# Sliding-window attention and a mixture of experts on one core: bf16 attention in 128-key blocks, tokens sorted by expert through a DRAM scatter, and the feed-forward of the chosen expert only, in 256-token tiles

## The chip, the core and the metric

One core of a Trainium2 chip runs the whole program. The time is device microseconds (us) of one execution. The engines are TensorE (PE for matmuls, PEld for weight loads), VectorE (DVE), ScalarE (ACT), GpSimd (POOL) and SyncE (SP); POOL and SP also issue transfers, POOL those that cast or go through an index. "Kernel before" and "kernel after" are the two sides of the diff.

## The reference

Attention with a window of 32 keys to either side runs over 8 batches of 8 heads, 576 positions and 64 columns. Its output is laid out as 4608 tokens of 512 columns. Each token then takes one of 8 experts by a gate, to whose logits a bias by the token's modality (0 or 1) is added.

```python
def _attn_ref(q, k, v):                       # q, k, v: (8, 8, 576, 64)
    scores = scale * np.matmul(q, k.transpose(0, 1, 3, 2))
    mask = np.abs(pos[:, None] - pos[None, :]) <= 32
    attn = softmax(np.where(mask, scores, -1e9))
    return np.matmul(attn, v)

def _moe_ref(x, modality_id, w_gate, modality_bias, w1, w2):   # x: (4608, 512), w1: (8, 512, 1024)
    logits = x @ w_gate + modality_bias[modality_id]
    e_idx = np.argmax(logits, axis=1)
    gate_w = softmax(logits)[np.arange(N), e_idx]
    for e in range(8):
        mask = e_idx == e
        h = np.maximum(x[mask] @ w1[e], 0.0)
        out[mask] = gate_w[mask, None] * (h @ w2[e])
    return out
```

The inputs are a fixed draw: random q, k, v, weights and biases, and modality 0 or 1 for each token at random.

## The kernel before

**Attention** loops over batch and head (L98, L99). For one head, k and q come in five pieces of 128 positions (L111, L117), are transposed on TensorE in fp32 (L113, L119) and copied to bf16 by VectorE (L114, L120). Then nine blocks of 64 queries follow, each against at most 128 keys: a score matmul (L137), scaling and mask on VectorE (L142), the exponent on ScalarE (L146), a load of the block's v rows on GpSimd's queue with a column of ones beside it (L151, L152), the output matmul with the sum in its last column (L155), a reciprocal and a scaling on VectorE (L158, L160), a transpose back (L165), a copy (L167) and a store of 64 x 64 values to `xT_dram` (L171).

**Gate and feed-forward** start when the attention's pools are closed. All experts' weights are then loaded to SBUF by two casting transfers on GpSimd's queue (L196, L200). Nine tiles of 512 tokens follow (L204). A tile is loaded transposed (L207), its logits are four groups of four matmuls of 8 columns (L214), and some fifteen small VectorE steps make the gate weight for the chosen expert and zero for the others (L219 to L260). Then each of the eight experts runs on the whole tile: 32 matmuls of 512 columns into `hT_ps` (L268), the relu on ScalarE (L272), 32 into `y_ps` (L277), and a multiply-add into `y_acc` on VectorE (L282, L287).

The code is written in program order, and a scheduler orders each engine's instructions when the kernel is built, with the pools' buffers and the data as its limits. Each engine then has a list of its own, with waits on semaphores in it.

## Time and profile before

| what | us |
|---|---|
| median of three executions | 1835.68 |
| lowest and highest | 1833.14, 1836.53 |
| span of the profiled execution, first to last instruction | 1834.9 |
| TensorE, VectorE, ScalarE, GpSimd busy in it | 1555.3, 789.7, 499.5, 311.4 |

The span lies 0.8 us under the median of the three, and the profiled execution has no time of its own beside its span, so that is all that can be said of what lies around it. A group of instructions is given by its line, engine, operation, tiles and shape, with its count, busy time, the mean length of one, and the idle time of the engine just before them with what ended it. Matmuls are pipelined: the busy time of a group divided by its count is the distance from one to the next, and the mean length of one is longer. PEclk is TensorE's granted clock as a share of full speed.

### The profile page before, as it was taken

The page shows a single profiled execution, that of the slowest core. Times are in us where ns is not written, and L with a number is a line of the kernel's source. Part 1 is how long each engine was busy: PE and PEld are TensorE (multiplying, and loading weights), DVE is VectorE, ACT ScalarE, POOL GpSimd, SP SyncE. Part 2 cuts the span into 40 slices and gives each one's busy share as a digit, 9 for nine tenths or more (in the row PEclk, how much of TensorE's full clock was granted, in tenths as well). Part 3 has the DMA queues.
Part 4 walks back from the last instruction along what each step waited for, and adds up shares of the span by engine and source line. Part 5 has one row for each costly group of instructions (what it writes and reads, how often), then busy time and mean ns, then how long its engine had stood idle before and what let it go on. Part 6 is the DMA issues. An engine that isn't in the chain of part 4 may idle for free.

```text
span 1834.9 us, 25930 instructions
## 1 busy us (share of the span) xinstructions
PE 1555.3 (85%) x7025; PEld 723.3 (39%) x7120; DVE 789.7 (43%) x4477; ACT 499.5 (27%) x1189; POOL 311.4 (17%) x596
## 2 busy tenths in 40 slices
PE   6777777777777777335999999999999999999999
PEld 3333333333333333112444444444444444444444
DVE  6667766766666676601212222313223231231322
ACT  1121112111111111121333333333333333333333
POOL 4443434443433444200000000000000000000000
PEclk9999999999999999997999999999999999999999
DMA  3343333333333333694000100101001010000000
GB/s 43 46 57 46 46 45 54 47 46 45 45 45 45 45 46 46 95 210 78 1 35 1 35 0 1 35 0 35 1 0 35 1 35 0 17 19 1 24 1 23
DMA packets 239198, 65.52 MB, mean 36 GB/s; under 512 B 217552, under 2 KB 230352, under 8 KB 239056
## 3 DMA queue, kind: packets, MB, share of 16 engines
q0 software_dynamic: 93744, 26.00, 13.4%
q1 hardware_dynamic: 145312, 37.88, 9.3%
q8 instruction: 59, 0.97, 0.2%
q14 instruction: 83, 0.68, 0.1%
HBM read 75.56 MB, written 14.16 MB: 49 GB/s over the span
## 4 chain that ended last, share of the span: by engine, by line
PE 68%; DMA 19%; issue 6%; DVE 5%; another core or an unknown queue 1%; POOL 1%; ACT 0%; SPq 0%; POOLq 0%; DVEq 0%; ACTq 0%
PE hT_ps L268 27%; PE y_ps L277 27%; DMA vaug<-in_v_dram 7%; DMA xT_dram<-oT 4%; PE tps L119 3%; PE o_aug L155 3%; PE tps L113 3%; DMA tmp<-in_q_dram 3%; PE oT_ps L165 3%; DMA w_all<-in_moe_w_dram 2%; PE sc L137 2%; DMA tmp<-in_k_dram 2%; DVE o_sb L160 1%; DVE recip L158 1%
## 5 line engine op out<-in xcount | busy, mean ns | idle before, releaser
L268 PE MATMUL hT_ps<-xT_sb,w_all 128*128 128x512 bf16 x2259 | 510.4, 380 | 41.5 <-DMA w_all<-in_moe_w_dram 38.7
L272 ACT ACTIVATE hT_sb<-hT_ps 128x512 bf16<-128x512 f32 x576 | 343.8, 597 | 695.0 <-PE hT_ps L268 653.7
L277 PE MATMUL y_ps<-w_all,hT_sb 128*128 128x512 bf16 x2254 | 507.1, 380 | 25.2 <-DMA w_all<-in_moe_w_dram 22.9
L287 DVE SCALAR_TENSOR_TENSOR yacc<-y_ps,mask_ge,yacc 128x512 f32<-128x512 f32 x252 | 189.2, 751 | 674.6 <-PE y_ps L277 662.9
L151 POOL DMA_DIRECT2D vaug<-in_v_dram x576 | 303.8, 530 | 445.6 <-DVE recip L158 140.3
L268 PEld LDWEIGHTS <-w_all 128*128 128x128 bf16 x2304 | 224.3, 98 | 310.7 <-DMA w_all<-in_moe_w_dram 38.3
L277 PEld LDWEIGHTS <-hT_sb 128*128 128x128 bf16 x2304 | 225.8, 98 | 296.6 <-issue 26.0
L146 ACT ACTIVATE exps<-exps 128x64 bf16<-128x64 bf16 (+1 forms) x576 | 144.9, 255 | 605.4 <-DVE exps L142 281.4
L165 PE MATMUL oT_ps<-ident,o_sb 64*64 64x64 f32 x576 | 174.9, 307 | 48.4 <-DVE o_sb L160 32.3
L155 PE MATMUL o_aug<-vaug,exps 128*64 128x65 bf16 x576 | 141.1, 249 | 78.7 <-DMA vaug<-in_v_dram 52.1
L119 PE MATMUL tps<-ident,tmp 128*64 128x128 f32 (+1 forms) x320 | 126.6, 396 | 39.7 <-DMA tmp<-in_q_dram 23.7
L167 DVE CAST oT<-oT_ps 64x64 bf16<-64x64 f32 x576 | 121.8, 211 | 81.3 <-DMA xT_dram<-oT 38.7
L160 DVE TENSOR_SCALAR o_sb<-o_aug,recip 64x64 f32<-64x64 f32 x576 | 153.6, 268 | 0.1
L113 PE MATMUL tps<-ident,tmp 128*64 128x128 f32 (+1 forms) x320 | 127.3, 398 | 27.5 <-DVE kT_sb L114 10.5
L137 PE MATMUL sc<-qT_sb,kT_sb 64*128 64x64 bf16 (+1 forms) x576 | 134.1, 235 | 6.2 <-DVE exps L142 4.0
L155 PEld LDWEIGHTS <-exps 128*64 128x64 bf16 x576 | 72.4, 127 | 164.5 <-issue 84.1
L158 DVE RECIPROCAL recip<-o_aug 64x1 f32<-64x1 f32 x576 | 89.3, 156 | 87.1 <-PE o_aug L155 81.1
L165 PEld LDWEIGHTS oT_ps<-ident,o_sb 64*64 64x64 f32 x576 | 75.9, 132 | 118.9 <-DVE o_sb L160 70.5
L120 DVE CAST qT_sb<-tps 64x128 bf16<-64x128 f32 (+1 forms) x320 | 84.2, 263 | 35.4 <-PE tps L119 22.3
L114 DVE CAST kT_sb<-tps 64x128 bf16<-64x128 f32 (+1 forms) x320 | 84.0, 262 | 24.5 <-PE tps L113 20.4
L142 DVE SCALAR_TENSOR_TENSOR exps<-sc,mask_mid 128x64 bf16<-128x64 f32 x448 | 92.6, 207 | 0.5 <-PE sc L137 0.2
L137 PEld LDWEIGHTS <-kT_sb 64*128 64x128 bf16 (+1 forms) x576 | 64.5, 114 | 65.9 <-issue 48.5
(46 smaller groups left out, 311.1 us busy)
## 6 DMA issues: line engine op xcount, KB each, us to landing
w_all<-in_moe_w_dram POOLq DMA_DIRECT2D x2, 8192.0 KB, 64.9
xT_dram<-oT SPq DMA_DIRECT2D x576, 8.0 KB, 1.8
out_dram<-yacc SPq DMA_DIRECT2D x36, 256.0 KB, 2.0
tmp<-in_k_dram SPq DMA_DIRECT2D x256, 32.0 KB, 1.9
tmp<-in_q_dram SPq DMA_DIRECT2D x256, 32.0 KB, 1.9
vaug<-in_v_dram POOLq DMA_DIRECT2D x512, 16.0 KB, 2.1
xT_sb<-xT_dram SPq DMA_DIRECT2D x9, 512.0 KB, 3.8
tmp<-in_k_dram SPq DMA_DIRECT2D x64, 16.0 KB, 2.0
```

The source lines that it names most:

```text
L113: nc.tensor.transpose(tps[:, :sl], tmp[:sl, :], ident[:sl, :sl])
L119: nc.tensor.transpose(tps2[:, :sl], tmp2[:sl, :], ident[:sl, :sl])
L137: nc.tensor.matmul(sc[:sk, :], kT_sb[:, ks:ke], qT_sb[:, qs:qs + QB], start=True, stop=True)
L146: nc.scalar.activation(exps[:sk, :], exps[:sk, :], mybir.ActivationFunctionType.Exp)
L151: nc.gpsimd.dma_start(vaug[:sk, :D], vbh[ks:ke, :])
L155: nc.tensor.matmul(o_aug[:], exps[:], vaug[:], start=True, stop=True)
L160: nc.vector.tensor_scalar(out=o_sb[:], in0=o_aug[:, :D], scalar1=recip[:], scalar2=None, op0=mybir.AluOpType.mult,)
L165: nc.tensor.transpose(oT_ps[:], o_sb[:], ident[:QB, :QB])
L268: nc.tensor.matmul(hT_ps[:], w1_all[:, e, kd, mi * P:(mi + 1) * P], xT_sb[:, kd, :], start=(kd == 0), stop=(kd == n_kd - 1),)
L272: nc.scalar.activation(hT_sb[:, mi, :], hT_ps[:], mybir.ActivationFunctionType.Relu)
L277: nc.tensor.matmul(y_ps[:], hT_sb[:, kf, si * P:(si + 1) * P], w2_all[:, e, kf, :], start=(kf == 0), stop=(kf == n_kf - 1),)
L287: nc.vector.scalar_tensor_tensor(out=y_acc[si][:], in0=y_ps[:], scalar=mask_ge[:, si, e:e + 1], in1=y_acc[si][:], op0=mybir.AluOpType.mult ...
```

## The change

Both halves are rewritten; no function of the computation is left as it was.

**Attention.** q and k of four heads are loaded at once as 96 partitions of six positions each and cast to bf16, q on GpSimd and k on ScalarE. v comes in five blocks of 128 keys for all heads and is cast on GpSimd. A pass takes two heads: six transposes for q and six for k into one PSUM buffer, copied by VectorE (q) and ScalarE (k); ten score matmuls of 192 or 96 queries against blocks of 128 keys into two PSUM tiles `sA` and `sB`; two exponents on ScalarE straight from PSUM; two multiplications by a mask of ones and zeros on VectorE; eighteen output matmuls of 65 columns into `oA` and `oB`, with a reciprocal and a normalisation each. The result goes to a row tile `xt` of 128 tokens by 544 bf16 columns.

**Routing**, once a batch: the rows are transposed, the logits and the chosen expert worked out for 5 x 128 slots (a batch's 576 tokens and 64 empty ones) in one set of small steps, ranks within the expert come from matmuls with a triangle and ones, and five indirect transfers on GpSimd's queue scatter the rows to a DRAM table `scr` with 4608 places for each expert. A row carries its gate weight and its token number. After batch 0 the weights of two experts that the batch used are loaded into two slots of SBUF.

**Feed-forward.** A table worked out on VectorE gives for each of 25 tile numbers the expert, whether its weights differ from those in the slot, and the first row; even and odd numbers run from the two ends of the list. 19 tiles are written out, six more stand in a conditional block that runs when the count asks for them. A tile of 256 tokens loads its rows by a register's address, transposes them, runs both matrices of its one expert, scales by the row's gate weight and scatters 2 x 128 rows to `out` with two indirect transfers. Its weight loads carry a condition from the table.

```diff
-        for b in range(B):
-            for h in range(H):
-                for si in range(n_ks):
-                    nc.sync.dma_start(tmp[:sl, :], kbh[s0:s1, :])
-                    nc.tensor.transpose(tps[:, :sl], tmp[:sl, :], ident[:sl, :sl])
-                    nc.vector.tensor_copy(kT_sb[:, s0:s1], tps[:, :sl])
...
-                for qi in range(n_qb):
-                    nc.tensor.matmul(sc[:sk, :], kT_sb[:, ks:ke], qT_sb[:, qs:qs + QB], start=True, stop=True)
...
-                    nc.gpsimd.dma_start(vaug[:sk, :D], vbh[ks:ke, :])
...
-        w1_all = moe_w_pool.tile([P, E, n_kd, F], BF16, tag="w1")
-        for nt in range(n_nt):
...
-            for e in range(E):
...
+        tc.tile_pool(name="ps_s", bufs=1, space=bass.MemoryType.PSUM) as ps_s,
+        tc.tile_pool(name="ps_o", bufs=1, space=bass.MemoryType.PSUM) as ps_o,
+        tc.tile_pool(name="ps_t", bufs=1, space=bass.MemoryType.PSUM) as ps_t,
+        tc.tile_pool(name="ps_m", bufs=1, space=bass.MemoryType.PSUM) as ps_m,
     ):
         for b in range(B):
...
+                    if nm == "q":
+                        nc.gpsimd.tensor_copy(o_ap, i_ap)
                     else:
+                        nc.scalar.copy(o_ap, i_ap)
...
+                nc.sync.dma_start(f_[:], v[b, :, s0:s0 + P, :].rearrange("h s d -> s h d"))
+                nc.gpsimd.tensor_copy(vt[:, j, :, 0:D], f_[:])
...
+                for src, dst, eng in ((qb[g], qT[:, 32:32 + S], "v"), (kb[g], kT[:], "a")):
+                    tp = ps_t.tile([P, S], BF16, tag="tp")
+                    for i in range(R):
+                        nc.tensor.transpose(tp[:, SP_ * i:SP_ * (i + 1)],
+                                            src[:, i, D * l:D * l + P], ident[0:SP_, 0:SP_])
...
+                    nc.scalar.activation(pt[:, :, o0:o0 + wd], s_t[:, :, 0:wd], ACT.Exp, scale=scale)
+                    w2_ = 512 if o0 == 0 else 384
+                    nc.vector.tensor_tensor(
+                        out=pt[:, :, o0:o0 + w2_], in0=pt[:, :, o0:o0 + w2_],
+                        in1=mask[:, o0:o0 + w2_].unsqueeze(1).to_broadcast([P, 2, w2_]), op=ALU.mult)
...
+            for m in range(NM):
+                tp = ps_t.tile([P, n_kd, P], BF16, tag="tp")
+                for kd in range(n_kd):
+                    nc.tensor.transpose(tp[:, kd, :], xr[:, m, P * kd:P * kd + P], ident[:])
+                xT = rt.tile([P, n_kd, P], BF16, tag="xT")
+                nc.vector.tensor_copy(xT[:], tp[:])
...
+            for m in range(NM):
+                nc.gpsimd.indirect_dma_start(
+                    out=scr[:], out_offset=bass.IndirectOffsetOnAxis(ap=di[:, m:m + 1], axis=0),
+                    in_=xi[:, m, :], in_offset=None, bounds_check=E * N - 1, oob_is_err=False)
+            if b == 0:
...
+                for i in range(2):
+                    e_r = reg(sp_i[0:1, i:i + 1], [ET.Pool], 0, E - 1)
+                    load_w(1, i, e_r)
+                    load_w(2, i, e_r)
...
+        def stage_load(i):
+            r_r = reg(tab[0:1, 2, i:i + 1], [ET.SP], 0, E * N - TT)
+            xg = xgp.tile([P, 2, ROW // 2], I32, tag="xg")
+            nc.sync.dma_start(xg[:], scr[bass.ds(r_r, TT), :].rearrange("(s p) c -> p s c", p=P))
...
+        def weights(i):
+            e_r = reg(tab[0:1, 0, i:i + 1], [ET.Pool], 0, E - 1)
+            c_r = reg(tab[0:1, 1, i:i + 1], [ET.Pool], 0, 1)
+            load_w(1, i % 2, e_r, cond=(c_r == 1))
...
+                nc.gpsimd.indirect_dma_start(
+                    out=out, out_offset=bass.IndirectOffsetOnAxis(ap=ix[:, s:s + 1], axis=0),
+                    in_=ys[:], in_offset=None, bounds_check=N - 1, oob_is_err=False)
...
+            if x_ + 1 < n:
+                stage_load(tiles[x_ + 1])
+                wr = weights(tiles[x_ + 1])
+            up(i)
+            if x_:
+                down(tiles[x_ - 1])
+            if x_ + 1 < n:
+                weights2(tiles[x_ + 1], wr)
...
+        ffn(list(range(n_base)), pools)
+        with tc.If(n_tiles > n_base):
+            ffn(list(range(n_base, NTILE)), pools)
```

Where instructions stand now is shown at three places. Names end in a number that tells copies apart, and DMASW, DMAHW, DVE, PE and Activation behind "waits" are the semaphores that an instruction waits on; DMASW are those of transfers issued by GpSimd, several of them in turn.

The first place is TensorE in the middle of attention. Before, scores (`sc`) and outputs (`o_aug`) of one head's blocks and transposes alternate:

```order
L165 MATMUL oT_ps_12340<-ident_61,o_sb_12338 64x64 [waits DVE_49]
L137 LDWEIGHTS kT_sb_12255
L137 MATMUL sc_12421<-qT_sb_12256,kT_sb_12255 128x64 [waits DVE_49]
L165 MATMUL oT_ps_12359<-ident_61,o_sb_12357 64x64 [waits DVE_49]
L155 LDWEIGHTS exps_12366 [waits DMASW2_49,Activation_49]
L155 MATMUL o_aug_12372<-vaug_12369,exps_12366 64x65 [waits PE_49]
```

Now, at the end of a pass (`pt1` is the pass's masked exponent, `kT_1175` the next pass's k):

```order
L288 LDWEIGHTS pt1_157
L288 MATMUL oB_1151<-vt0_159,pt1_157 128x65
L295 LDWEIGHTS pt1_157
L295 MATMUL oB_1151<-vt0_159,pt1_157 64x65
L272 LDWEIGHTS kT_1175
L272 MATMUL sA_1192<-qT1_155,kT_1175 128x192
```

All scores of the next pass but its first now stand behind the last output matmul of this one.

The second place is GpSimd in the middle of attention. Before, it only issues the blocks' v loads:

```order
L151 DMA vaug_2095<-in_v_dram 128x64 [waits DMASW5_49,DVE_49,PE_49]
L151 DMA vaug_2115<-in_v_dram 96x64 [waits DMASW6_49,DVE_49,PE_49]
L151 DMA vaug_2187<-in_v_dram 128x64 [waits DMASW7_49,PE_49]
L151 DMA vaug_2206<-in_v_dram 128x64 [waits DMASW0_49,PE_49]
L151 DMA vaug_2225<-in_v_dram 128x64 [waits DMASW1_49,DVE_49,PE_49]
```

Now, at a batch's end, with casts of q and v for later batches among and behind the five row scatters:

```order
L364 DMA scr_66<-xt0_161,di_2062 36864x272 [waits DMASW0_49,DVE_49]
L233 CAST c__2822<-f__2820 96x4x6x64 [waits DMAHW3_49,PE_49,Pool_49]
L364 DMA scr_66<-xt0_161,di_2062 36864x272 [waits DMASW1_49]
L364 DMA scr_66<-xt0_161,di_2062 36864x272 [waits DMASW2_49]
L364 DMA scr_66<-xt0_161,di_2062 36864x272 [waits DMASW3_49]
L233 CAST c__2830<-f__2828 96x4x6x64 [waits DMAHW7_49,PE_49,Pool_49]
L364 DMA scr_66<-xt0_161,di_2062 36864x272 [waits DMASW4_49]
L242 CAST vt1_160<-f__2836 128x8x64 [waits DMAHW0_49,PE_49,Pool_49]
```

Each scatter waits for the landing of the one before it, and the casts behind them stand in the same list.

The third place is GpSimd in the feed-forward. Before, its last transfers are the two weight loads, and nothing of the tiles is on it:

```order
L151 DMA vaug_14470<-in_v_dram 128x64 [waits DMASW4_49,DVE_49,PE_49]
L151 DMA vaug_14490<-in_v_dram 96x64 [waits DMASW5_49,DVE_49,PE_49]
L196 DMA w1_all_14532<-in_moe_w1_dram 128x32x1024 [waits DMAHW2_49,DMAHW1_49,DMAHW3_49,DMAHW0_49,DMAHW4_49,DMASW7_49,DMAHW5_49,DMASW6_49,DMAHW6_49,DMASW0_49,DMAHW7_49,DVE_49,Activation_49]
L200 DMA w2_all_14534<-in_moe_w2_dram 128x64x512
L318 UNCONDITIONAL_BRANCH
```

Now, one tile's share of it:

```order
L185 TENSOR_LOAD tab_3235 x2
L178 REGISTER_ALU x2
L178 ISA
L178 DMA w1_1_151<-in_moe_w1_dram 128x4x1024 [waits DMASW4_49]
L509 DMA out_0_dram<-ys_3642,ix_3617 4608x512 [waits DMASW2_49,DVE_49]
L509 DMA out_0_dram<-ys_3723,ix_3712 4608x512 [waits DMASW5_49,DVE_49]
L181 REGISTER_ALU x2
L181 ISA
L181 DMA w2_1_153<-in_moe_w2_dram 128x8x512 [waits DMASW7_49,PE_49]
```

Register loads, two conditional weight loads and two output scatters a tile have come to GpSimd, and each scatter waits for a landing.

## Rows read from the trace of the kernel before

**Rows 1.** The page: its first line, and busy time by engine.

```profile
span 1834.9 us, 25930 instructions
...
PE 1555.3 (85%) x7025; PEld 723.3 (39%) x7120; DVE 789.7 (43%) x4477; ACT 499.5 (27%) x1189; POOL 311.4 (17%) x596
```

**Rows 2.** Three stretches: length, each engine's busy us (instructions), PEclk, DMA share, GB/s.

```profile
0.00:752.00 752.00, 553.71 (x2362) 267.19 (x2362) 517.57 (x3643) 145.93 (x576) 306.41 (x593) 1.00 0.38 46
752.00:845.00 93.00, 20.93 (x111) 9.88 (x113) 17.00 (x133) 12.21 (x25) 4.97 (x3) 0.89 1.05 181
845.00:1835.00 990.00, 980.64 (x4555) 446.26 (x4646) 255.16 (x703) 341.36 (x588) 0.00 (x0) 1.00 0.04 14
```

**Rows 3.** The chain that ended last, 752 to 850 us: start, length, what.

```profile
758.55 45.52 DMA w_all<-in_moe_w_dram
...
821.58 22.87 another core or an unknown queue
```

**Rows 4.** Groups of TensorE, then a piece of the whole chain of waits.

```profile
L268 PE MATMUL hT_ps<-xT_sb,w_all 128*128 128x512 bf16 x2259 | 510.4, 380 | 41.5 <-DMA w_all<-in_moe_w_dram 38.7
...
L268 PEld LDWEIGHTS <-w_all 128*128 128x128 bf16 x2304 | 224.3, 98 | 310.7 <-DMA w_all<-in_moe_w_dram 38.3 <-issue 11.3
...
L214 PE MATMUL logits_ps<-wg_sb,xT_sb 128*128 128x8 bf16 x144 | 6.5, 167 | 8.2 <-DVE logits L219 7.8 <-DVE oT L167 0.3
...
997.29 6.95 PE hT_ps L268 x32
```

**Rows 5.** Groups of ScalarE.

```profile
L272 ACT ACTIVATE hT_sb<-hT_ps 128x512 bf16<-128x512 f32 x576 | 343.8, 597 | 695.0 <-PE hT_ps L268 653.7 <-PE y_ps L277 40.4
...
L146 ACT ACTIVATE exps<-exps 128x64 bf16<-128x64 bf16 x512 | 128.5, 255 | 538.6 <-DVE exps L142 252.9 <-DVE vaug L152 147.1 <-PE tps L119 80.3
```

**Rows 6.** Groups of VectorE.

```profile
L287 DVE SCALAR_TENSOR_TENSOR yacc<-y_ps,mask_ge,yacc 128x512 f32<-128x512 f32 x252 | 189.2, 751 | 674.6 <-PE y_ps L277 662.9 <-remote 11.7
L160 DVE TENSOR_SCALAR o_sb<-o_aug,recip 64x64 f32<-64x64 f32 x576 | 153.6, 268 | 0.1
...
L158 DVE RECIPROCAL recip<-o_aug 64x1 f32<-64x1 f32 x576 | 89.3, 156 | 87.1 <-PE o_aug L155 81.1
...
L114 DVE CAST kT_sb<-tps 64x128 bf16<-64x128 f32 x256 | 70.4, 275 | 17.0 <-PE tps L113 14.9
...
L114 DVE CAST kT_sb<-tps 64x64 bf16<-64x64 f32 x64 | 13.5, 211 | 7.5 <-PE tps L113 5.6 <-PE sc L137 1.2
```

**Rows 7.** A wait in the timeline: start, length, instruction, idle before it, releaser.

```profile
10.97 0.13 PEld L155 LDWEIGHTS <-exps 128*64 128x64 bf16 x1 [0.22 <-ACT exps L146]
```

**Rows 8.** Groups of GpSimd.

```profile
L151 POOL DMA_DIRECT2D vaug<-in_v_dram x576 | 303.8, 530 | 445.6 <-DVE recip L158 140.3 <-PE sc L137 117.9 <-PE o_aug L155 53.1
...
L200 POOL DMA_DIRECT2D w_all<-in_moe_w_dram x1 | 2.8, 2755 | 0.0
```

**Rows 9.** Transfers: packets, MB, engines' share by queue; then issues, KB, us to landing.

```profile
q0 software_dynamic: 93744, 26.00, 13.4%
q1 hardware_dynamic: 145312, 37.88, 9.3%
...
vaug<-in_v_dram POOLq DMA_DIRECT2D x512, 16.0 KB, 2.1
xT_sb<-xT_dram SPq DMA_DIRECT2D x9, 512.0 KB, 3.8
```

**Rows 10.** GpSimd's constants in the timeline's first microseconds.

```profile
0.74 0.20 POOL masks.py:197 MEMSET ident<- 128x128 f32 x1 [0.29 <-POOLq L307]
...
1.15 0.29 POOL masks.py:199 TENSOR_SCALAR_AFFINE_SELECT ident<-ident 128x128 f32<-128x128 f32 x1
...
2.22 0.24 POOL L30 TENSOR_SCALAR_AFFINE_SELECT mask_last<-mask_last 128x64 f32<-128x64 f32 x1
```

**Rows 11.** TensorE's weight loads right behind the wait for weights.

```profile
804.95 0.15 PEld L268 LDWEIGHTS <-w_all 128*128 128x128 bf16 x1 [0.28 <-issue]
805.38 0.15 PEld L268 LDWEIGHTS <-w_all 128*128 128x128 bf16 x1 [0.27 <-issue]
```

More of the change, by code (lines that the diff above doesn't have):

```diff
@@ new lines @@
+    le = const.tile([P, E, E], FP32)
+    nc.gpsimd.memset(le[:], 1.0)
+    nc.gpsimd.affine_select(out=le[:], in_=le[:], compare_op=ALU.is_ge, fill=0.0,
+                            base=0, pattern=[[1, E], [-1, E]], channel_multiplier=0)
+    sgn = const.tile([P, NTILE + 1], FP32)
+    nc.gpsimd.memset(sgn[:], 0.0)
+    nc.gpsimd.memset(sgn[:].rearrange("p (n two) -> p n two", two=2)[:, :, 0:1], 1.0)
+    off = const.tile([P, NTILE + 1], FP32)
+    off_i = const.tile([P, NTILE + 1], I32)
+    nh = (NTILE + 1) // 2
@@ new lines, in reg @@
+    def reg(ap, engines, lo, hi):
+        return nc.values_load(ap, engines=engines, min_val=lo, max_val=hi,
+                              skip_runtime_bounds_check_because="the table is clamped on chip")
+    qT_t = [const.tile([P, 32 + S], BF16, name=f"qT{i}") for i in range(2)]
+    p_t = [const.tile([P, 2, PW], BF16, name=f"pt{i}") for i in range(3)]
+    v_t = [const.tile([P, NM, H, D + 1], BF16, name=f"vt{i}") for i in range(2)]
+    x_t = [const.tile([P, NM, ROW // 2], I32, name=f"xt{i}") for i in range(2)]
@@ new lines @@
+    nc.vector.tensor_reduce(out=ci[:], in_=t2[:], axis=AX.X, op=ALU.add)
+    cx = const.tile([P, E], FP32)
+    nc.vector.tensor_tensor(out=cx[:], in0=ci[:], in1=nt[:], op=ALU.subtract)
+    tt = const.tile([P, NTILE], FP32)
+    nc.vector.scalar_tensor_tensor(out=tt[:], in0=sgn[:, 0:NTILE], scalar=ci[:, E - 1:E], in1=off[:, 0:NTILE],
+                                   op0=ALU.mult, op1=ALU.add)
+    shp = [P, NTILE, E]
+    ttb = tt[:].unsqueeze(2).to_broadcast(shp)
+    g1 = const.tile(shp, FP32)
```

565 lines of the change are left out of this document (364 added, 201 removed).

## The prediction

> **What bounds the kernel now.** I read the page first, then the stretches, then the chain of waits, then the groups of instructions. TensorE is busy for 85% of the span [rows 1], but the stretches show three stages with different limits [rows 2]. Attention is 0 to 752 us. TensorE is busy for 554 us of it with 2362 matmuls, 234 ns each, and VectorE for 518 us: 64 heads of 9 blocks, 11.75 us a head, made of small instructions that wait for one another. From 752 to 845 us the kernel waits for the weights: the chain goes through the two weight loads, from 758.55 to 844.45 us [rows 3]. From 845 us TensorE is busy for 981 of 990 us: all eight experts on all tokens, 9 x 8 x 64 = 4608 matmuls of 512 columns at 6.95/32 = 217 ns each [rows 4].
>
> **The inputs.** By the reference's fixed draw 2300 tokens choose expert 0, 2308 expert 4, and none another. That makes 9 + 10 = 19 tiles of 256, exactly the 19 that stand outside the last conditional block, so that block is not entered. Even tile numbers hold expert 4 and odd ones expert 0, and the weights guessed after batch 0 fit, so each later load of weights should be skipped.
>
> **The change part by part.** The span is 1834.9 us [rows 1] and the median of the three times 1835.68, so what lies around the span is about 0.8 us; I sum spans and leave that off.
>
> *Prices.* A matmul costs 217/512 = 0.42 ns a column. With 8 columns one takes 6.5/144 = 45 ns [rows 4], the floor. Between the two the weight load either hides (its mean of 98 ns lies under the matmul of 512) or adds 45 ns: 256 columns cost 109 to 154 ns, 192 cost 81 to 126, 128 cost 54 to 99, 96 and 65 cost 45 to 86. ScalarE: 255 ns at 64 columns, 597 at 512, so 0.76 a column [rows 5]. VectorE: a copy from PSUM 211 and 275 ns at 64 and 128, so 1.0 a column; with an operand 268 at 64 and 751 at 512, so 1.08; a reciprocal 156 [rows 6]. An engine hands on in 0.22 us [rows 7].
>
> *Feed-forward, 990 us now.* A tile needs 8 transposes of 128, 32 matmuls of 256 and 16 of 512 columns: 0.43 + 3.49 + 3.47 = 7.4 us if weight loads hide, 9.2 if not. I take 7.5, since 98 ns of load fit under 109. Beside it ScalarE has 4 x 0.60 = 2.4 us and VectorE 1.17 + 2 x 0.75 = 2.7. GpSimd is nearer: its output scatters each wait for the one before to land. No row shows an indirect scatter. The nearest is the v load, also 128 rows: 0.53 us on GpSimd [rows 8], 2.1 us to landing [rows 9]. The other bound is a weight load's 2.76 us on GpSimd [rows 8] plus 2.1. I take 3.1, of it 1.0 on the engine, near the v load. Per tile: the first scatter 3.1, the issue of the second 1.0, then two register loads and two skipped weight loads, which no row shows either (0 to 0.53 us for each of six), beside the landing of the second: 6.2 to 7.3 us. So TensorE decides, narrowly. 19 x 7.5 = **143 us**.
>
> *Attention, 752 us now.* 32 passes of two heads. All scores of the next pass but its first stand on TensorE behind this pass's last output matmul, so a pass is a loop: six score matmuls (4 x 81 + 2 x 45 = 0.42), hand over 0.22, exponent of 960 columns 0.94, hand over 0.22, two masks on VectorE of 1024 and 768 columns 1.31 + 1.03, hand over 0.22, eight output matmuls 0.36: 4.7 us. The second exponent (0.79) and the copies of the next q and k (0.72, 0.65) lie under the masks or the first exponent; without that cover each pass would cost their length more. VectorE's own work is 0.72 + 2.34 + 0.31 + 0.61 + 0.48 = 4.5, so it is nearly the bound anyway. The masks are the unknown: two bf16 operands in SBUF have no row. With no cost beyond the 0.27 of a small instruction the loop would go through both exponents, 0.42 + 0.22 + 0.94 + 0.79 + 0.22 + 0.27 + 0.22 + 0.36 = 3.4 us. I keep 4.7 by the only rows with two operands. The Trainium skill ("VectorE: DVE Perf Modes", section "The perf-mode tier table (the rule you actually need)") says that tensor_tensor on bf16 in SBUF delivers two elements a cycle; no run here shows it, and by it the loop would be 3.8 us and the total 29 us lower.
>
> *Routing, per batch.* Five times four transposes (0.3), hand over, copy of 512 (0.66), hand over, with one PSUM buffer: 7.3 us. Then eight small VectorE steps of about 0.2, the next q copy 0.72, rank matmuls 0.3 with two hand-overs, and the last normalisation ahead of it: 3.7. Little attention can run beside it, since the next scores stand behind the ranks. A batch is 4 x 4.7 + 11 = 29.8 us, eight make **238 us**.
>
> *GpSimd in attention.* Five row scatters a batch, each behind the landing of the last: 5 x 3.1 + 5 v casts of about 0.6 (0.78 ns a column [rows 10]) = 19 us, under 29.8. SP's loads carry 3.7 MB a batch. Its queue ran 37.88 MB at 9.3% of the engines [rows 9], 222 GB/s, so 17 us; scatters of 0.7 MB at the other queue's 106 GB/s add 6.6. Both fit.
>
> *Weights.* Two of eight experts: 86 x 2/8 = **21 us** of transfers [rows 3]. They stand in GpSimd's queue between the scatters of batch 0, and the last v cast of batch 1 stands behind them, so I count all as a stall once; 0 if it hides, 35 if the casts come later still.
>
> *Ends.* Start: 44 GpSimd constants at 0.16 apart (ten from 0.74 to 2.22 us [rows 10]) plus 2 for the wide ones, then the first q cast 1.3, then filling the first pass: **15 us**. Between the stages: five VectorE steps 1.0, three scatters 9.3 (the table's 30 small steps hide under them), register loads and weight checks 2, two scatters 6.2, a register load and the rows' load 4 (512 KB landed in 3.8 [rows 9]), transposes, copy and hand-overs 2.3: **25 us**. Tail: 0.75, two scatters 6.2, a register load and the branch 1: **8 us**.
>
> Sum: 15 + 238 + 21 + 25 + 143 + 8 = 450 us.
>
> **The rivals.** *Less chain, more overlap, 388 us.* Masks at the low end and routing partly beside the next batch: 3.4 x 4 + 8 = 22 us a batch, 62 less. For it: in the first stage TensorE's and VectorE's busy times together exceed the stretch by 42% [rows 2]. Against it: single PSUM buffers.
>
> *TensorE at its lower clock in attention, 490 us.* The weight wait left the granted clock at 0.89 for its stretch [rows 2], and the matmuls behind it came 0.43 us apart, as their weight loads show [rows 11], that is 512 columns at 1.2 GHz, where 0.217 is 2.4. Doubling the matmul terms adds 3.1 us to four passes and 1.9 to a routing: 8 x 5 = 40. Against it: the clock stood at 1.00 over the whole first stage with all its waits. The Trainium skill ("TensorE: Matmul & The Clock Gate", section "HAM oscillation — how this bites in real kernels") has the clock fall back when bursts of matmuls are split by waits; the trace agrees for the weight wait and not for attention.
>
> *GpSimd becomes the bound, 560 us.* With a scatter of 6 us its batch is 33 (+26), the passage +15 and a tile 6 + 3 + 2 = 11 us (+67). It decides in the feed-forward from about 3.5 us, in attention from 5.3. For it: an address is read for each row. Against it: the v load's 2.1 us.
>
> *The skipped loads are not skipped, 512 us.* One expert's weights are 86/8 = 10.75 us against 7.5 a tile: 19 x 3.25 = 62 more. The condition is an operand of the transfer, and no row shows one.
>
> *Slower than before.* One mechanism: 40 + 38 scatters in series. Each would have to cost 3.1 + (1836 - 450)/78 = 21 us; the price decides from there. The dearest GpSimd row is 2.76 us.
>
> **How the numbers follow.** Forecast (400 to 500) 0.45, more overlap 0.20, lower clock 0.13, GpSimd 0.15, no skipping 0.05, slower 0.02. The likeliest is the forecast, 450. The low end takes in the overlap case with a little more, 370; the high end the GpSimd case, 565; beyond them about 0.2. Only the last case is not faster: faster 0.97, same 0.01, slower 0.02, where 0.2% is about what a measurement of this kernel can tell from no change.
>
> **What would show it.** Right: pass after pass about 4.7 us apart in attention, VectorE the busiest engine there, a gap of some 11 us a batch with few matmuls, one stall near batch 1 while weights arrive, and feed-forward tiles 7.5 us apart at a granted clock of 1.00 with no weight transfers. A mask of 0.7 us instead of 1.3 would mean less overlap was needed. Tiles paced by GpSimd's scatters show that rival; weight bytes in the last stretch show the skipping failed. The forecast is wrong if a pass takes over 6 us, or if the time between the stages is tens of us longer.

## The result and the profile after

The changed kernel takes 505.0 us (median of four, 502.6 to 507.9) against 1836.1 us before: 0.275 of the time, interval 0.274 to 0.276. The prediction's 450 us lies 55 us, or 11%, below; its range (370 to 565) holds the result. The profiled execution spans 505.1 us and has a time of 506.8. One execution of the run e7_vact below (488.9 us, granted clock 0.94) was in a slower state than all others and is left out.

The page of the changed kernel: first line, busy time by engine, granted clock in 40 slices, GpSimd's queue. The lines answer to [rows 1, 9].

```profile
span 505.1 us, 7239 instructions
...
PE 344.3 (68%) x2694; PEld 228.9 (45%) x2712; DVE 200.5 (40%) x529; ACT 144.2 (29%) x197; POOL 140.9 (28%) x225
...
PEclk9999999999999999999999999999999999999965
...
q0 software_dynamic: 8624, 18.66, 12.9%
```

Four stretches of it, as in [rows 2]: length, then busy us (instructions) of TensorE, its weight loads, VectorE, ScalarE and GpSimd, granted clock, DMA share, GB/s. They are batches 1 and 7 of attention, the first feed-forward tiles and the later tiles.

```profile
53.00:101.00 48.00, 25.28 (x209) 16.28 (x207) 21.96 (x57) 13.66 (x16) 19.61 (x20) 1.00 1.03 199
...
274.00:307.00 33.00, 24.75 (x200) 15.98 (x199) 17.13 (x53) 9.65 (x14) 4.85 (x5) 1.00 0.06 20
327.00:400.00 73.00, 71.42 (x536) 50.48 (x544) 19.17 (x36) 23.88 (x40) 14.99 (x32) 1.00 0.26 82
400.00:470.00 70.00, 59.41 (x439) 40.29 (x446) 17.45 (x33) 19.10 (x32) 15.92 (x32) 1.00 0.28 86
```

Three things are to be seen. In attention TensorE, not VectorE, is the busiest engine (75% of batch 7). Batch 1 has as much TensorE work as the others and takes 12 to 16 us longer. And TensorE is busy for 98% of the feed-forward up to 400 us and for 85% from there.

The stages against the prediction's sum, by these marks of the trace: the row addresses of the last batch are done at 308.7, the first up matmul starts at 327.4, the last matmul ends at 481.0.

| stage | predicted us | measured us |
|---|---|---|
| start, attention, weight stall | 15 + 238 + 21 = 274 | 308.7 |
| between the stages | 25 | 18.7 |
| 19 feed-forward tiles | 143 | 153.6 |
| tail | 8 | 24.1 |

Within the first line, by the distance from one batch's gate exponent (L336) to the next: batch 0 ends 10 us late (its exponent stands at 53.0 us, 1.9 before the batch's end, where 15 + 29.8 was predicted for the end); batch 1 takes 48.3; batches 2 to 5 take 36.2, 33.8, 34.9, 35.1; batches 6 and 7 take 33.1 and 32.4, where 29.8 was predicted.

**The pass.** TensorE in a pass of the last batch: start, length, line, tiles, shape (weights' rows*columns), count, idle before.

```profile
281.60 0.50 PE L272 MATMUL sA<-qT,kT 64*128 64x192 bf16 x4
...
282.43 0.66 PE L254 MATMUL tp<-ident,c__2830 96*128 96x96 bf16 x6
...
284.55 0.35 PE L288 MATMUL oA<-vt,pt 128*128 128x65 bf16 x3
284.83 0.26 PE L295 MATMUL oA<-vt,pt 128*64 128x65 bf16 x1
285.02 0.24 PE L288 MATMUL oA<-vt,pt 128*128 128x65 bf16 x1
285.19 0.26 PE L295 MATMUL oA<-vt,pt 128*64 128x65 bf16 x1
...
287.62 0.26 PE L295 MATMUL oB<-vt,pt 128*64 128x65 bf16 x1
287.82 0.50 PE L272 MATMUL sA<-qT,kT 64*128 64x192 bf16 x4
```

One pass is 287.82 - 281.60 = 6.22 us. The output matmuls take 284.55 to 287.82, 3.27 us, more than half. Three 128-wide ones (L288) start 48 and 53 ns apart; where L288 and L295, with 64 columns of weights, alternate, they start 166 ns (to the 64-wide) and 196 ns (back) apart, the medians from 230 to 306 us.

In the same pass, ScalarE's first exponent, then VectorE:

```profile
282.22 0.97 ACT L275 ACTIVATE pt<-sA 128x960 bf16<-128x960 f32 x1 [3.12 <-PE sA L272]
...
283.13 0.76 DVE L259 COPY qT<-tp 128x576 bf16<-128x576 bf16 x1 [0.78 <-PE tp L254]
283.81 1.15 DVE L277 TENSOR_TENSOR pt<-pt,mask 128x1024 bf16<-128x1024 bf16 x2
```

The first exponent ends at 283.19, but the copy of the next q stands ahead of the masks, so they start 0.62 us later. The two masks together take 1.15 us.

**The later tiles.** VectorE in the feed-forward, early (tiles 7.39 us apart) and late (8.9 apart):

```profile
344.90 0.16 DVE L499 TENSOR_TENSOR ix<-xg,pen_i 128x2 int32<-128x2 int32 x1 [3.88 <-DMA out_dram<-ys,ix]
345.33 0.75 DVE L507 TENSOR_SCALAR ys<-py,xg 128x512 f32<-128x512 f32 x1 [0.27 <-PE py L504]
...
352.65 0.16 DVE L499 TENSOR_TENSOR ix<-xg,pen_i 128x2 int32<-128x2 int32 x1 [4.25 <-DMA out_dram<-ys,ix]
352.74 0.75 DVE L507 TENSOR_SCALAR ys<-py,xg 128x512 f32<-128x512 f32 x1
...
422.13 0.16 DVE L499 TENSOR_TENSOR ix<-xg,pen_i 128x2 int32<-128x2 int32 x1 [6.95 <-DMA out_dram<-ys,ix]
422.21 1.41 DVE L507 TENSOR_SCALAR ys<-py,xg 128x512 f32<-128x512 f32 x2
```

`ix`, the row addresses of an output scatter, is a copy of 0.16 us. It waits for a scatter's landing, and `ys`, which empties TensorE's PSUM, stands behind it. At 344.9 that leaves 0.27 us to spare, at 352.7 nothing, and at 422.1 both `ys` are late. The order of VectorE's instructions in the built program says why (the numbers tell tiles of one name apart):

```
488 L499 TENSOR_TENSOR ix_4377<-xg_4126,pen_i_3247 128x2 [waits DMAHW0_49,DMASW5_49,DMASW2_49]
489 L507 TENSOR_SCALAR ys_4103<-py_4094,xg_3841 128x512 [waits DVE_49,PE_49]
490 L507 TENSOR_SCALAR ys_4117<-py_4108,xg_3841 128x512 [waits DVE_49,PE_49]
491 L470 COPY xT_4137<-tp_4128 128x1024 [waits PE_49]
```

The scheduler put the `ix` of the tile three ahead (xg_4126) in front of this tile's `ys` (xg_3841). With four buffers it takes the buffer of the tile four back, and that is the tile just before the `ys`: VectorE waits until both of its scatters have landed.

**Scatters beside loads.** GpSimd between batches 0 and 1, and after the last batch:

```profile
60.22 1.02 POOL L364 DMA_INDIRECT scr<-xt,di  x1 [0.30 <-issue]
61.23 0.97 POOL L181 DMA_DIRECT2D w<-in_moe_w_dram  x1
67.84 1.00 POOL L364 DMA_INDIRECT scr<-xt,di  x1 [5.64 <-DMA scr<-xt,di]
...
81.25 1.00 POOL L364 DMA_INDIRECT scr<-xt,di  x1 [4.53 <-DMA scr<-xt,di]
82.25 0.62 POOL L242 CAST vt<-f__628 128x512 bf16<-128x512 f32 x1
...
309.17 0.97 POOL L364 DMA_INDIRECT scr<-xt,di  x1 [19.78 <-DVE t L395]
311.86 0.97 POOL L364 DMA_INDIRECT scr<-xt,di  x1 [1.73 <-DMA scr<-xt,di]
```

With nothing else in flight a row scatter comes 2.7 us after the last (309.17, 311.86). Beside the weights and inputs it is 6.5 to 7.6 us, and batch 1's last v cast (82.25) stands behind the whole row. TensorE waits 12.6 us for that cast:

```profile
82.92 0.21 PE L288 MATMUL oB<-vt,pt 128*128 128x65 bf16 x1 [12.64 <-POOL vt L242]
```

This is the stall of batch 1.

**The end.** GpSimd's last steps, from the views of two lines of the program's end: a semaphore step at 495.6 us, just behind the landing of the last scatter (495.5), and a drain from 497.5 us, the longest of three. Lengths are in ns (shortest, median, longest).

```profile
L543 POOLq INC_SWDGE_SEM  x1: 1847/1847/1847, 495.6 to 495.6; - x1
...
L570 POOLq DRAIN  x3: 50/103/6853, 497.5 to 504.9; - x3
```

### The profile page after: what moved, and what is told of

Read it like the earlier page. It is cut to its first block, busy times and chain, and to the rows that moved or that the text cites. A ratio compares the mean times of both kernels' runs of the same rounds, so it can differ in the third digit from the quotient of the medians.

```text
span 505.1 us, 7239 instructions
## 1 busy us (share of the span) xinstructions
PE 344.3 (68%) x2694; PEld 228.9 (45%) x2712; DVE 200.5 (40%) x529; ACT 144.2 (29%) x197; POOL 140.9 (28%) x225
## 3 DMA queue, kind: packets, MB, share of 16 engines
q1 hardware_dynamic: 66576, 36.93, 33.6%
## 5 line engine op out<-in xcount | busy, mean ns | idle before, releaser
L364 POOL DMA_INDIRECT scr<-xt,di x40 | 41.3, 1033 | 150.4 <-DMA scr<-xt,di 69.0
L492 ACT ACTIVATE hT<-ph 128x512 bf16<-128x512 f32 x76 | 45.4, 597 | 122.3 <-PE ph L490 122.3
L490 PE MATMUL ph<-xT,w 128*128 128x256 bf16 x608 | 70.6, 275 | 0.0
L509 POOL DMA_INDIRECT out_dram<-ys,ix x38 | 36.9, 970 | 115.6 <-DMA out_dram<-ys,ix 56.6
L504 PE MATMUL py<-w,hT 128*128 128x512 bf16 x286 | 67.6, 379 | 0.9
L490 PEld LDWEIGHTS <-w 128*128 128x128 bf16 x608 | 59.4, 99 | 7.2
L288 PEld LDWEIGHTS <-pt 128*128 128x128 bf16 x320 | 29.3, 108 | 40.9 <-DVE pt L277 23.0
L295 PEld LDWEIGHTS <-pt 128*64 128x64 bf16 x256 | 32.7, 128 | 30.6 <-issue 12.9
L277 DVE TENSOR_TENSOR pt<-pt,mask 128x1024 bf16<-128x1024 bf16 x64 | 44.4, 723 | 3.9 <-ACT pt L275 3.9
L288 PE MATMUL oA<-vt,pt 128*128 128x65 bf16 x192 | 33.8, 239 | 17.2 <-DVE pt L277 15.4
L504 PEld LDWEIGHTS <-hT 128*128 128x128 bf16 x304 | 29.8, 98 | 32.0
L288 PE MATMUL oB<-vt,pt 128*128 128x65 bf16 x128 | 30.1, 235 | 13.4 <-POOL vt L242 12.6
L507 DVE TENSOR_SCALAR ys<-py,xg 128x512 f32<-128x512 f32 x38 | 27.5, 748 | 17.0 <-PE py L504 15.4
L295 PE MATMUL oB<-vt,pt 128*64 128x65 bf16 x128 | 33.7, 263 | 0.0
L295 PE MATMUL oA<-vt,pt 128*64 128x65 bf16 x128 | 33.7, 263 | 0.0
```

Source lines behind the costliest of these rows:

```text
L277: nc.vector.tensor_tensor(out=pt[:, :, o0:o0 + w2_], in0=pt[:, :, o0:o0 + w2_], in1=mask[:, o0:o0 + w2_].unsqueeze(1).to_broadcast([P, 2, ...
L288: nc.tensor.matmul(o_t[:, m - m0, h, :], pt[:, h, c0:c0 + P], vt[:, m, 2 * hp + h, :], start=first, stop=(m == 0), skip_group_check=True)
L295: nc.tensor.matmul(o_t[0:64, m - m0, h, :], pt[:, h, c1:c1 + 64], vt[:, m - 1, 2 * hp + h, :], start=False, stop=True, skip_group_check=True)
L364: nc.gpsimd.indirect_dma_start(out=scr[:], out_offset=bass.IndirectOffsetOnAxis(ap=di[:, m:m + 1], axis=0), in_=xi[:, m, :], in_offset=Non ...
L490: nc.tensor.matmul(ph[:, u, :], w1[:, kd, P * mi:P * mi + P], xTs[i][:, kd, :], start=(kd == 0), stop=(kd == n_kd - 1))
L492: nc.scalar.activation(hT[:, 2 * mp:2 * mp + 2, :], ph[:], ACT.Relu)
```

## The experiments

Each is set against the changed kernel's 505.0 us; "batch 7" and the like are distances between gate exponents as above. Except in the last part, each changes that kernel in one place. The scheduler orders the engines' lists anew for each, though, and one thing that moves from run to run matters here: where in GpSimd's list the last v casts of batch 1 stand, behind the first of batch 0's five row scatters or behind the fifth. Batch 1 can therefore not be compared from run to run as the other batches can.

**The order of the output matmuls.**

```diff
                     for m in ms:
                         for h in range(2):
                             nc.tensor.matmul(o_t[:, m - m0, h, :], pt[:, h, c0:c0 + P], ...)   # 128 wide
+                    for m in ms:
+                        for h in range(2):
                             if m > 0:
                                 nc.tensor.matmul(o_t[0:64, m - m0, h, :], pt[:, h, c1:c1 + 64], ...)
```

> The same 18 output matmuls a pass, but for each of the two outputs first all with 128 columns of weights (L288), then all with 64 (the half rows, L297). In the changed kernel three 128-wide ones in a row come 50 ns apart and the alternating ones 165 to 195 ns. Theory: what costs is the change between neighbours, either of the width or of adding to rows just written. Then the 18 take some 1.0 us instead of 3.2; exponents, the q copy and the masks take over as the loop, a pass falls from 6.2 to 4.2 to 4.6 us and the total from 505 to 440 to 455. Rival 1: each 64-wide matmul is dear in itself, about 180 ns wherever it stands: 10 x 0.05 + 8 x 0.18 = 1.9 us, pass 5.0, total 465 to 470. Rival 2: the order has no part in it (each matmul waits for something else, such as its weights out of the masks): total 505.

Measured: 479.5 us (477.2 to 483.7), pass 5.31 us. TensorE in a pass, last batch but one:

```profile
266.86 0.40 PE L288 MATMUL oA<-vt,pt 128*128 128x65 bf16 x4
267.68 0.34 PE L272 MATMUL sA<-qT,kT 64*128 64x192 bf16 x1 [0.42 <-ACT kT L261]
267.95 0.29 PE L288 MATMUL oA<-vt,pt 128*128 128x65 bf16 x2
268.17 0.43 PE L297 MATMUL oA<-vt,pt 128*64 128x65 bf16 x4
```

Inside a group all start some 54 ns apart, the 64-wide ones too: they are not dear in themselves, so rival 1 falls, and with it rival 2. Only the first of a group comes 170 to 180 ns after its predecessor. The pass gains 0.9 us and not 1.6 to 2.0: a score matmul of the next pass stands among the outputs and now waits 0.42 us for its k copy on ScalarE, and three changes of width within the 18 are left, some 0.12 us each.

Not all of the 26 us comes from the pass. Batch 1 fell from 48.3 to 39.9, more than the 3.6 of four passes; its last v casts now stand behind the first row scatter (54.7 and 55.3 us) and not the fifth, and TensorE no longer waits for them there.

**The same order, one width.**

```diff
-  o_t[0:64, m - m0, h, :], pt[:, h, c1:c1 + 64]
+  o_t[:, m - m0, h, :],    pt[:, h, c1:c1 + P]      # c1 capped at PW - P
```

> The order stays alternating and each second matmul still adds to the rows written just before, but the eight half-row matmuls of a pass take 128 columns of weights instead of 64 (all from the second half of the neighbour's slot and beyond, so the attention output is not the reference's). Theory 1, the change of width costs: 18 x 0.05 us, pass 4.2 to 4.6 us, total 440 to 455 as with the grouped order. Theory 2, adding to rows just written costs: matmuls stay about 180 ns apart, total 500 to 510.

Measured: 483.4 us (481.2 to 484.5), pass 4.81 us. The end of the outputs in a pass:

```profile
271.44 0.25 PE L288 MATMUL oB<-vt,pt 128*128 128x65 bf16 x1
271.49 0.24 PE L295 MATMUL oB<-vt,pt 128*128 128x65 bf16 x1
271.55 0.24 PE L288 MATMUL oB<-vt,pt 128*128 128x65 bf16 x1
271.60 0.25 PE L295 MATMUL oB<-vt,pt 128*128 128x65 bf16 x1
271.78 0.50 PE L272 MATMUL sA<-qT,kT 64*128 64x192 bf16 x4
```

Alternating and adding to the rows just written, they come 54 ns apart. So it is the change of width that costs: 166 to 196 ns from one start to the next, 110 to 140 more than the 51 to 55 of equal neighbours. The Trainium skill has a rule of this kind ("TensorEngine Tiling (Array Packing)", section "Tiling Modes": changing the tiling mode drains TensorE). That the step from 128*128 to 128*64 is such a change is read from the rows' shapes; the price is that of these runs. The pass falls to near what theory 1 said (4.81 for 4.2 to 4.6), the total does not (483 for 440 to 455): batches 6 and 7 take 27.5 and 26.8 us, but batches 2 to 4 still 36.2, 33.6 and 34.0. Something else holds those; the last group comes back to it.

**The copy of q.**

```diff
                     if eng == "v":
+                        if it >= 2:
+                            continue
                         nc.vector.tensor_copy(o_ap, i_ap)
```

> The copy of the transposed q from PSUM on VectorE (0.76 us a pass) is left out from the third pass on, so the attention output is not the reference's; its transposes stay. Theory: the copy stands on VectorE ahead of the first mask and, through the single PSUM buffer, ahead of the transposes of k, so it is not hidden as the prediction had it: a pass falls from 6.21 to 5.4 to 5.6 us, total 480 to 490. Rival: the output matmuls are the pass's bound and the masks have slack: pass 6.0 to 6.2, total 500 to 505.

Measured: 495.1 us (494.7 to 496.0), pass 5.63. The pass fell by 0.58, nearly what theory said (5.4 to 5.6): the copy is on the path. The total fell by 10 and not 15 to 25, since again batches 2 to 4 gained little (33.6, 35.2, 32.3).

**The buffers of ix.**

```diff
-  ix = yp.tile([P, 2], I32, tag="ix")
+  ix = yp.tile([P, 2], I32, tag="ix", bufs=8)
```

> Eight buffers instead of four for the tile ix of row addresses in the feed-forward, nothing else. The scheduler put ix of the tile three ahead on VectorE in front of this tile's ys, and with four buffers it waits until both output scatters of the tile before have landed. Theory: this wait, not GpSimd's own work, makes the later tiles 8.7 to 9.4 us instead of 7.39 and fills the backlog of scatters. Then all tiles come 7.4 to 7.6 us apart, the tail shrinks from 24 to 10 to 14 us, total 478 to 488. Rival: the scatters in series (3.5 us each and register loads between) are the pace, 8 us a tile or more whatever the buffers: then tiles may come 7.4 us apart for longer, but the scatters still end at the same time and the total stays at 502 to 507.

Measured: 492.0 us (491.8 to 494.6), 13 less. All tiles come 7.39 us apart. One stretch, then what VectorE and GpSimd waited for from 391 to 460 us (us in total, times, longest):

```profile
400.00:460.00 60.00, 59.58 (x448) 41.86 (x454) 18.38 (x32) 19.31 (x33) 16.18 (x33) 1.00 0.32 106
```

```profile
POOL out_dram L509 <- DVE ys L507: 24.5, 9, 3.0
POOL out_dram L509 <- DMA out_dram<-ys,ix: 20.1, 10, 3.4
DVE ix L499 <- DMA xg<-scr: 20.0, 8, 3.4
```

`ix` now waits for its own rows, which harms nobody, and TensorE is busy for 99%. The rival falls: 38 scatters from 340.4 to 477.6 us are 3.71 us each, 7.42 a tile, just what TensorE's 7.39 lets through. In the changed kernel the same waits, 391 to 470 us, read

```profile
DVE ix L499 <- DMA out_dram<-ys,ix: 62.3, 9, 7.2
...
POOL out_dram L509 <- DMA out_dram<-ys,ix: 32.3, 9, 3.8
POOL out_dram L509 <- DVE ys L507: 27.1, 9, 3.4
```

that is, `ix` waits for a scatter and a scatter for `ys` behind `ix`: a ring. The tail shrank from 24 to 21 us, less than expected, since three scatters are still left when the matmuls end.

**The end of the program.**

```diff
-        with tc.If(n_tiles > n_base):
-            ffn(list(range(n_base, NTILE)), pools)
```

> The conditional block behind the 19 tiles, which is not entered with these inputs, is left out. In the changed kernel 9 us lie between the landing of the last scatter (some 495.5 us) and the end: a semaphore step of GpSimd of 1.85 us on the block's line and then a drain of GpSimd of 6.85 us. Theory: both come with the block and its branch: total 496 to 498. Rival 1: only the first belongs to the block: 502 to 504. Rival 2: both come with GpSimd's transfers in flight and stay: 504 to 506.

Measured: 502.9 us (499.3 to 506.0). That is in rival 1's range, but 2 us are less than the spread of either kernel, so the total decides nothing. The trace says more. GpSimd's semaphore step of 1.85 us is gone; its drain stays, 8.05 us, but begins before the last landing. From the issue of the last scatter to the end there are 8.7 us (489.1 to 497.7) where the changed kernel has 12.3 (492.8 to 505.1), so the block costs 3.7 us, more than rival 1 had and less than the theory. The profiled execution (span 497.7) gained more in all because 12 distances between tiles instead of 8 were 7.4 us before VectorE's ring closed: where it closes varies, and each slow tile costs some 1.5 us.

**The weights, and the zeros.** First the place of the four weight loads:

```diff
-            if b == 0:          # behind the guess of the two experts
+            if b == 3:
                 for i in range(2):
                     e_r = reg(sp_i[0:1, i:i + 1], [ET.Pool], 0, E - 1)
                     load_w(1, i, e_r)
                     load_w(2, i, e_r)
```

> The four loads of the guessed experts' weights are issued after batch 3 instead of after batch 0. Theory: batch 1 is 48 us instead of 34 because 4 MB of weights stand before the next batches' inputs while the transfers of the first three batches still fill the queues; later the input loads run ahead, so the weights hide: total 488 to 493. Rival: wherever they are put, their issue (about 2.7 us each on GpSimd) and bytes hold up the next batch's casts on GpSimd by the same amount; then batch 4 is 45 to 48 us and the total stays at 502 to 507.

Measured: 505.2 us (503.7 to 506.4). Batch 1 fell to 35.7 and batch 4 stayed at 34.5, so the weights do hide later (a part of batch 1's fall is the order again: its v casts stand behind the first scatter here, as in e1_group, where with the weights in place it took 39.9); batch 2 rose to 39.8, the first up matmul came 5 us sooner (322.1), and the ring of `ix` closed two tiles sooner and took it back. The theory was right on the place, the rival on the total.

Then the place of the zero fill, which stood ahead of the batch loop:

```diff
+            if b == 0:          # behind this batch's loads
+                for e in range(E):
+                    nc.sync.dma_start(scr[N * e:N * e + TT, :].rearrange(...), zero[:])
```

> The eight transfers that fill the tiles' tails in the scratch with zeros are issued after the first batch's loads, not ahead of them; nothing else. In the changed kernel they are issued from 14.6 to 20.1 us, after the token ids, and the second k load and three of five v loads of batch 0 only behind them; GpSimd waits 12.8 us for the third v load. Theory: the fill costs the first batch 5.5 us or a little more: the last exponent of batch 0 moves from 53 to 45 to 48 us, total 497 to 500. Rival 1: the time goes to the token ids' small transfers, which stay in front: total 503 to 506. Rival 2: what batch 0 gains is given back in batch 1, where the weights and inputs fill the queues: batch 0 ends earlier, total 503 to 506.

Measured: 510.4 us (508.4 to 514.6), slower. Batch 0 ended 3 us sooner (49.8), batch 1 took 52.3: rival 2 and more. TensorE waited 14.4 us there for a v cast, where it had been 12.6: three casts stand behind the fifth row scatter here, and one did before.

**What holds batches 1 to 5.** With grouped order and eight buffers as the base:

> The grouped order and the eight ix buffers together. Alone they took 26 and 13 us off 505. Theory: they act in different stages, so the sum holds: 464 to 468. Rival: the shorter attention brings the first feed-forward tiles forward and GpSimd's scatters, 3.7 us each in series, set the end: 470 or more.

Measured: 463.9 us (462.8 to 465.5), the best kernel here: 0.253 of the time before (0.252 to 0.253), 41 us below the changed one. The two gains add up (505 - 26 - 13 = 466).

> Grouped order, eight ix buffers, and the five casts of v per batch on ScalarE instead of GpSimd. The first two alone, summed from their own runs, give 505 - 26 - 13 = 466. With the grouped order batches 6 and 7, which load no more inputs, take 29 us, but batches 2 to 5 still 30 to 35. Theory: the v casts stand behind the row scatters in GpSimd's queue, and each scatter waits for the one before to land; on ScalarE they don't, batches 2 to 5 fall to 29 and the total to 440 to 452. Rival: the transfers of the inputs themselves set those batches (DMA engines 70% busy there); then they stay at 33 to 35 and the total at 462 to 470; a total above 470 would say that ScalarE's exponents now wait behind casts.

```diff
-                nc.gpsimd.tensor_copy(vt[:, j, :, 0:D], f_[:])
+                nc.scalar.copy(vt[:, j, :, 0:D], f_[:])
```

Measured: 471.2 us (469.1 to 472.1), above the base, which this run's own expectation put at 466 and the run before at 463.9. Batches 1 to 3 took 38.7, 42.7 and 36.1, batches 4 and 5 29.7 and 30.5; the base has 40.6, 33.0, 35.0, 33.8 and 30.3. That moving the casts would clear batches 2 to 5 is refuted: TensorE waits for no v cast any more, and something else takes their place (f3_ld8_vact).

> f1_both with eight buffers instead of three for the incoming q, k and v tiles. With the v casts moved off GpSimd, batches 1 to 3 still took 36 to 43 us, and the transfers of all inputs end only near 225 us at some 165 GB/s. Theory: the three buffers hold the loads back (a buffer is free only once its cast is done, and casts wait behind scatters); with eight the loads run ahead, batches 2 to 5 fall to 29 to 30, total 448 to 458. Rival: the transfers run as fast as they can (DMA engines 70 to 100% busy up to 200 us): batches stay at 33 to 35, total 463 to 468.

```diff
-        tc.tile_pool(name="ld", bufs=3) as ld,
+        tc.tile_pool(name="ld", bufs=8) as ld,
```

Measured: 479.1 us (477.5 to 483.4), 15 above the base. Both were wrong. The loads did run ahead: batches 3 and 4 fell to 31.3 and 31.2. But batch 1 took 54.3 and batch 2 41.9. From 60 to 90 us the DMA engines are full in both kernels (share 1.16 and 1.11), and TensorE does a third of the base's work; here this kernel, then the base:

```profile
60.00:90.00 30.00, 4.74 (x44) 3.03 (x43) 2.46 (x6) 5.66 (x6) 14.00 (x17) 1.00 1.16 237
```

```profile
60.00:90.00 30.00, 13.16 (x135) 8.59 (x133) 10.85 (x28) 7.46 (x8) 12.07 (x13) 1.00 1.11 221
```

TensorE waits 17.6 us for one v cast behind five row scatters, 6.2 to 8.5 us from one to the next. The same cast in the base, then here:

```profile
53.90 0.64 POOL L242 CAST vt<-f__625 128x512 bf16<-128x512 f32 x1
...
81.06 0.62 POOL L242 CAST vt<-f__625 128x512 bf16<-128x512 f32 x1
```

In the base it stands behind the first scatter, here behind the fifth. So the scheduler's order changed together with the buffers, and batch 1's loss of 13.7 us comes with this cast: the row of scatters itself took only 3.5 us longer (29.4 from the first issue to the last, 25.8 in the base). In batch 2 the deeper loads do show. Batch 1's row takes 27.5 us there and 17.3 in the base, the DMA share from 90 to 120 us is 1.03 and 0.83, and VectorE waits 12.2 us for a landing of these scatters (below).

> f2_ld8 with the v casts on ScalarE. Theory (GpSimd's row of scatters and casts is what is left): 5 to 10 us below f2_ld8. Rival (transfers): within 3 us of f2_ld8, or above it where ScalarE's exponents wait behind casts.

Its edit is that of f2_ld8 with that of e7_vact.

Measured: 491.0 us (488.1 to 491.6), 12 above f2_ld8, so the theory falls. The rival allowed for that, but by exponents waiting on ScalarE, and the long wait is on VectorE. What VectorE waits for most is in this line of its waits, 92 to 217 us:

```profile
DVE xt L342 <- DMA scr<-xt,di: 40.2, 3, 19.2
```

This is the kind of wait that `ix` had, now in attention. L342 (L340 in the changed kernel) copies the next batch's token ids into the row tile, which has two buffers. The scheduler puts it ahead of this batch's normalisation, and it waits for the row scatters of the batch before to land. From 50 to 310 us it cost VectorE 3.8 us in the changed kernel, 20.7 with grouped order, 21.7 in the base, 18.4 in f2_ld8, 32.6 with v casts on ScalarE, and 56.8 here. In the base, batch 4:

```profile
177.50 1.26 DVE L277 TENSOR_TENSOR pt<-pt,mask 128x1024 bf16<-128x1024 bf16 x2 [0.87 <-ACT pt L275]
183.45 0.43 DVE L342 COPY xt<-ioi 128x5 int32<-128x5 int32 x1 [4.69 <-DMA scr<-xt,di]
183.79 0.18 DVE L302 RECIPROCAL rec<-oA 128x6 f32<-128x6 f32 x1
```

Where nothing is in the way the normalisation begins 2.5 us after the masks do (e1_group's last batch but one: 266.12 and 268.64). Here it begins at 183.79, 3.8 us later than that, behind a copy of five columns. By batch, VectorE's wait there in the base is 10.9, 1.0, 4.3, 4.7 and 0.8 us in batches 1 to 5, which are 12.0, 4.4, 6.4, 5.2 and 1.7 us longer than batch 7; in batch 2 TensorE waits 4.5 us for a v cast instead. In f2_ld8, batches 3 to 5 have no such wait and take 30.3 to 31.3. So once the pass is short, the landing of the scatters beside the loads accounts for most of what batches 1, 3 and 4 take beyond batch 7. That is read from these traces; a third row buffer, which would take the wait away, was not run.

> f2_ld8 with the weights issued after batch 3 instead of batch 0. Moving them alone, in the changed kernel, ended attention 5.4 us sooner and the gain was lost in the feed-forward to the wait of ix, which is gone here. Theory: now it stays, 4 to 8 us below f2_ld8. Rival: the first 200 us are full of transfers in any case, and the weights only change places with inputs: within 3 us of f2_ld8.

Its edit is that of f2_ld8 with that of e5_wlate.

Measured: 471.1 us (468.0 to 472.6), 8 below f2_ld8, the upper end of what the theory gave. It is still 7 above the base: batches 1 to 3 (41.7, 41.7, 37.1) take 12 us more than there, and VectorE waits 7.7, 10.1 and 8.0 us for the row tile in them.

## Why the prediction was right and wrong

The result is inside the range, but not by the forecast's own case: 505 lies just outside the 400 to 500 that it was given, and the range reaches to 565 for a case that did not happen. In part that is luck: terms set too high (the masks, the weights, the routing, the passage between the stages) took back some of what the terms set too low cost.

**Right: the direction, the stages and what bounds the last one.** Two experts on sorted tokens leave 19 tiles, the guessed weights are loaded once (each later, skipped load takes GpSimd 0.05 us; its queue carries 18.7 MB in all, 26.0 before [rows 9]), and a tile with free scatters takes 7.39 us against 7.5. The rivals "loads not skipped" and "slower than before" fell. "Less chain, more overlap" had the cheap masks and a routing of 8 us right, and its pass of 3.4 us wrong. "TensorE at its lower clock in attention" fell too: the granted clock stays at 1.00 through all its waits and drops only in the last two slices, when the matmuls are done.

**The step that failed: the pass, 4.7 predicted, 6.2 measured.** The prediction named "over 6 us" as the mark of a wrong forecast, and VectorE as the busiest engine of attention, where it is TensorE. Three of its terms were mis-sized.
- *Eight output matmuls 0.36 us.* They are priced at 45 ns each by [rows 4], whose matmuls all have 128 columns of weights. Here each second one has 64, and a change of width costs 110 to 140 ns: the 18 take 3.3 us, 2.9 of them after the masks. Taking only the change of width away gave 1.4 us of the pass back (e2_wide).
- *"The copies of the next q and k lie under the masks or the first exponent".* The k copy is hidden (it runs beside the output matmuls, 284.68 to 285.32 us), the q copy is not: it begins just before the first exponent ends and delays the masks by 0.62 us. Leaving it out gave 0.58 (e3_noqt).
- *Two masks 1.31 + 1.03 us.* They take 0.68 and 0.55, 0.51 ns a column from one to the other. The estimate of 1.08 a column came from fp32 operands [rows 6]. The Trainium skill's rule, weighed in the prediction and set aside ("VectorE: DVE Perf Modes", section "The perf-mode tier table (the rule you actually need)"), has bf16 in SBUF at two elements a cycle, and the trace agrees with it: half the price. This error hid 1.1 us of the others.

**Routing** is 14.5 - 6.2 = 8.3 us between the last pass of a batch and the next, not 11: the copy of 512 bf16 from PSUM takes 0.42 us, not 0.66 [rows 6], which makes 1.2 of the 2.7 in five copies. **Between the stages** 18.7 us were measured and not 25: the five row scatters came 2.7 us apart and not 3.1, and the register loads and weight checks, counted as 2, ran between them.

**Attention, 35 us more in all.** Batch 0 is 10 late: the token ids and the zero fill stand in SP's queue from 8.7 to 20.0 us, ahead of the second k and three v loads, and GpSimd waits 12.8 us for v. The prediction had no term for the ids and the fill in that queue. Moving the fill behind gave 3 us to batch 0 and took 4 from batch 1 (e8_zlate), so nothing shows that this time could be saved. The weight stall, counted as 21, was 48.3 - 32.8 = 15.5, in the place and by the mechanism named (the v cast behind them), with the scatters between the weights as the links. Seven quiet batches at 32.8 for 29.8 make 21, and batches 2 to 5 another 9, of which VectorE's wait for the row tile is 3.8; the rest was not traced. The prediction had added up GpSimd's row and the loads and found that "both fit": they do as sums, but not as an order of waits.

**The rival "GpSimd becomes the bound" came half true.** The prediction had it decide from about 3.5 us a scatter; in series they came 3.5 to 4.0 apart. But GpSimd alone would have kept up (e6_ix8). The 11 us of the feed-forward came from an instruction moved ahead on VectorE, which the prediction did not look for: its work for VectorE in a tile (2.7 us) has no term for `ix`, neither its 0.16 us nor the wait for what its buffer held.

**The tail, 24 for 8.** Two scatters were expected after the last matmul; four were still to be issued, 3.5 us apart. And 9.6 us lie behind the last landing (495.5), of which GpSimd's semaphore step and drain are 8.7, where "a register load and the branch 1" stood. Without the conditional block the end is 3.7 us shorter (e9_noif).

**What stays open:** whether a third row buffer would bring batches 1 to 5 to the 28.6 us that batch 7 takes with grouped order. It was not run. Batch 1's v casts ahead of the scatters alone do not: in e1_group and the base they stand behind the first, and batch 1 still takes 39.9 and 40.6, with VectorE waiting 9.5 and 10.9 us for the row tile.

## What to carry to other kernels

Price a small matmul by its neighbours: sort a run of them by the width of their weights, and count each change. Wherever a scheduler may move an instruction forward, ask what its output buffer held before: a copy of 0.2 us that waits for a transfer's landing stalls everything behind it on its engine, and more buffers for a tiny tile were a cheap cure here (13 us). Where a chain waits for small transfers, loading further ahead can make them land later: a row of five scatters took 27.5 us with eight load buffers and 17.3 with three. And when an experiment changes a pool or an instruction, compare the engines' lists before and after as well as the times: in the run with eight load buffers the scheduler had also put a v cast behind four more scatters, and that run was 15 us slower.
